# Joint 128-row transfers for the last 64 rows of the modulation and of wk, wv and wq

## The chip, the cores and the metric

The kernel runs on one core of one Trainium2 chip. The metric is the time of one execution on the device in microseconds (us), as the median of the runs shown. Three engines compute beside TensorE (PE): VectorE (DVE), ScalarE (ACT) and GpSimd (POOL). SyncE (SP) issues nearly all transfers; they go to the core's 16 DMA engines.

## The reference, cut to what matters

One transformer block over 2048 tokens of width D = 576. A row `c` of 576 numbers is turned into six rows of modulation by `w_mod` (576 x 3456). The first two of them shift and scale the normalised input, and q, k and v are products of the result with `wqkv` (576 x 1728).

```python
mod = (_silu(c) @ w_mod).reshape(c.shape[0], 6, 1, -1)
sa, ca, ga, sb, cb, gb = (mod[:, 0], mod[:, 1], mod[:, 2], mod[:, 3], mod[:, 4], mod[:, 5])
h = _layernorm(x, axis=-1) * (1 + ca) + sa
x = x + ga * _A_ref(h, A_wqkv, A_wo)      # linear attention, 32 heads of 18
h = _layernorm(x, axis=-1) * (1 + cb) + sb
x = x + gb * _B_ref(h, B_w1, B_w2)        # silu MLP, 576 -> 4608 -> 576
```

The change concerns the start alone: the product with the first two pieces of `w_mod`, and the loads of `wqkv`.

## The kernel before

**Rows of 576.** 576 is 4 x 128 + 64, so each weight comes as four chunks of 128 rows and a tail of 64. Each float32 operand is split into a rounded part (`hi`, made by ACT in `w_hi`) and the rest (`lo`, made by DVE or POOL in `w_lo`), and a product takes three passes of PE: hi by hi, lo by hi and hi by lo. Of a tail of 64 rows hi and lo lie in one tile of 128 partitions, so that two passes do.

**The first stage.** `load_mod_cols` loads the first two pieces of `w_mod` in two sets of columns (0 to 255, then 256 to 575): four chunks of 128 rows, which hold both pieces, and the tail, whose 64 rows of piece 0 go to partitions 0 to 63 of `tmod` and those of piece 1 to partitions 64 to 127, with one transfer each. DVE sums the four chunks weighted by silu(c) (`mod_sum`), PE adds the tail (`mod_tail`) and the partitions (`mod_sums`, `mod_last`), and `col_a` takes shift and scale. The row c itself comes by two small loads on ACT's queue: 4 rows of 128 (L277), and its last 64 numbers twice, as a transfer of 1 x 2 x 64 (L278). Meanwhile the first four row tiles of x (`xt`, 128 tokens each) are normalised, turned by PE, modulated and split (`modulate`, `split_h`) into `hT`.

`load_w(j, ks)` loads wk (j = 0), wv (1) and wq (2) into `acc`, chunk by chunk; chunk k = KC = 4 is the tail of 64 rows, loaded by `load_rows` into partitions 0 to 63 of a tile of its own. Then ACT and DVE split them. PE makes k of the row tiles 0 and 1 (`k_part`, into `psK`), then v of tile 0 (`v_proj`), v of tile 1, then q of tiles 0 and 1, and from there on k, v and q tile by tile. The last two lo parts of wv that v of tile 0 waits for (chunk 3 and tail) are made by POOL.

**What sets the order.** PE's order in this stage is that of the code. For the other engines a scheduler orders the instructions, and the tables `ORDERS` (one for each engine, read by `arrange`) put the first 547 instructions of DVE, the first 425 of ACT, the first 119 of POOL and the first 153 of SP of the traced program in a given order. Each engine takes its instructions strictly in that order. The MLP's main part is ordered by a plan of its own.

**The tail's lines.** L293 loads the tail of the modulation, L236 the chunks of the weights, L238 their tails; L317 and L318 are `w_hi` of a chunk and of a tail, L323 and L325 `w_lo` of a chunk and of a tail.

Of the kernel before, what the change touches and what calls it, by code (L numbers as in the profile page):

```python
# [17 lines left out]
P = 128  # L18
# [5 lines left out]
def kernel(ctx: ExitStack, tc, A_x, A_wqkv, A_wo, B_x, B_w1, B_w2, c, w_mod, out):  # L24
# [7 lines left out]
    nc = tc.nc  # L32
    V, A, G, T = nc.vector, nc.scalar, nc.gpsimd, nc.tensor
# [3 lines left out]
    S, D = x.shape  # L37
# [6 lines left out]
    KC = D // P  # L44
# [3 lines left out]
    HALF = D // 2  # L48
# [4 lines left out]
    def f32(ap):  # L53
        return ap.bitcast(F32)
# [3 lines left out]
            0-106 114 107-109 115 110-113 116-1159 1162 1160 1163 1161 1164-2530  # L58
        """,
        "DVE": """  # L60
            0 3 2 1 4 6-7 11 8 12-13 9-10 14-16 18 17 5 19-22 30 23-24 28-29 25-27 43 31 44 33-34 36 35 37-38 32 39 41
            40 42 45-47 50 48-49 67-68 51-53 57 70 62 64 69 58-59 63 65 122 85-86 66 71-72 87 55 88 73 60 74 61 76-77
            75 78-79 89-90 56 80 83 81-82 91 84 123 54 93 97 96 98 100 94 99 92 124 95 101 103-104 107-108 105 102 125
            109-110 132-133 135 134 111 138 136-137 139 106 112 141-142 140 143-144 114 145-146 148-149 117 147 113
            115 126 118-119 116 120 128-129 131 121 192 150 195 193 196 151 194 198 130 199 152 158 153 197 201 200
            202-203 154 157 204 161 208 127 155 205 159 206 209 160 162 164 156 207 175-176 165 168 163 169 166 170
            177 171 178 173 172 167 179 174 182-183 185-186 184 187-188 191 189 210 216 211 190 219 212 215 213 217
            214 220 218 228-229 232 231 225 180 233 223 235 234 230 236 239 237 240 221 241 238 222 242 224 243
            245-247 244 248 251-252 249 253 250 227 254 257 255 258 256 226 261 259 262 265 267 266 268-270 263 260
            271-272 264 273-274 278-279 275-276 280-281 277 282 284 283 285-286 288-289 296 290-294 297 308-309 298  # L70
            295 299 317 300-301 318 302 310 312 311 327 303 287 328 313 336 319 314 337 320-322 315 181 304 329-330
            323-325 346 326 331-332 316 338 340 347 339 333 358 341 305 345 359 334 370 335 352 349 342-343 350-351
            356 371 348 379 344 306 353 307 354 360 380 362-363 390 361 355 368 364-365 391 372 366 373 369 374 367
            378 409 381-382 357 388 383 410 375 384 426 376 385 387 389 395-396 394 377 398 392 399 403 397 405 402
            386 393 415 413-414 427 416 400 417 406 401 418 435 423 428 424 407 425 419 429-430 436 408 420-421 434
            431 422 411 432 437 412 438 404 439 444 446-448 440 433 441 445 442 457 450-451 443 452-455 449 459 456
            460-462 466 463 458 465 467-468 482 469 471 486 483 473 464 488 470 489 472 494-495 484 496-497 491 485
            475 498 490 478 499 492 501 506 500 476-477 479 503 502 493 474 481 505 480 504 510 507 511 487 509 508
            513-514 516 512 515 517-521 523 522 524 527 525-526 529 528 532-533 531 540 536 535 537 534 541 538-539
            543-544 542 530 546 545  # L80
        """,
        "Activation": """
            0-2 4-6 9 7-8 10 3 11-12 16 19 13-14 18 17 15 21 26 20 27 22-23 29 24 28 25 30-31 35 32-33 36-37 46 48 39
            47 42 49 40 44 50 41 55 43 58 56-57 38 59-60 45 53 61 51 54 52 62 34 65 63 66-70 64 72 71 73-74 77-78 75
            79-82 76 83-85 93-96 87 86 98 88 99 101 100 97 89 102 104 90-91 103 92 105-107 111-113 108 116 109 117-118
            120 114 110 115 121 145-146 119 122 151 126-127 147 123-124 148 144 128-129 152 131 143 130 149 125 134
            132-133 135-136 150 154 153 138-139 137 140-141 160 155 161-162 156 142 165 157 166-167 158 168 163 159
            164 169-170 179 176-177 180-181 178 182 184-186 183 175 187-188 190 189 191-192 171 193-195 173 196 172
            197-198 200 199 201-203 205 174 206 204 208 210 209 207 212 211 213-217 219-220 222-223 218 221 225-226
            224 228 227 229-233 237 236 238 234 239-241 235 245-247 242 251 258 243 252 248-249 253 264 259 250 260  # L90
            271 254 256 261 265-266 257 255 262 267 269-270 274 272 268 283 263 276 275 294 273 278 277 279 297
            280-281 284-285 244 282 290-291 304 292-293 295-296 288 286-287 320 289 298-302 307 309-310 308 311 303
            305 312 323-324 313 316 331 314 306 317 315 319 327-328 332-333 329 318 330 334-335 326 336 321 325 322
            337 339 341-343 340 338 344-345 349-350 346-348 351 353 352 354-355 367 357 356 359 369 360 366 363 374
            361 364 375 358 362 371 380 365 381 377 372 382 376 383 378 373 379 368 384 370 386 385 390 387-388 392
            391 393 396 398 397 395 401 389 399-400 403-404 394 405 402 408 406 414 410-411 407 416 415 418 412 421
            417 422 419-420 409 413 424 423
        """,
        "Pool": """
            7-10 0 3 2 4-6 11-15 18 16-17 21 19-20 22 25 23 27 26 24 28-30 36 32 31 34 33 37 35 39 38 42 40 44 46 43  # L100
            45 41 48 51 47 49 53 55 52 54 50 66 56-57 69 58 61-62 59 67 65 63 71 60 70 68 72 64 73 75 74 80 85 81-82
            76-77 84 78 83 91 79 90 93 86 92 95-98 94 89 99 101 87 100 102 104 103 106 88 105 108 111 110 113 107 114
            109 116-117 112 115 118
        """,
        "SP": """
            0-25 30-31 26 28 27 29 32 39 33-34 40-43 35-38 53 44 71 54 72-73 55-56 45 74 46 58 47-48 57 59-60 75 61 77
            76 78 62 49 81 63-65 79 82-83 80 86 52 89 92 85 87 84 66 91 96 90 93 97-98 95 69 50 88 51 94 104 99 105
            101 67 100 103 70 102 107 68 109 108 114 106 110-111 116 113 115 118 124 117 119-121 126-127 123 112 122
            125 128 131 129 133 132 134-135 130 136-137 139 148 141 138 140 142-144 147 145-146 149-152
        """,  # L110
    }

# [33 lines left out]
    cols = {n: const.tile([P, KC + 1, 2], F32, name=f"col_{n}") for n in ("a", "b")}  # L146
# [6 lines left out]
    acc = [accb[t // 4][:, t % 4, :] for t in range(NT)]  # L153
# [14 lines left out]
    wq = wqp.tile([P, 2 * KC + 1, D], F32R, name="wq")  # L168
# [65 lines left out]
    def load_rows(raw, src, k):  # L234
        if k < KC:
            nc.sync.dma_start(raw, src[k * P : (k + 1) * P, :])  # L236
        else:
            nc.sync.dma_start(raw[0:64], src[KC * P : D, :])  # L238
# [49 lines left out]
    def load_mod_cols(k0, k1):  # L288
        c0, c1 = k0 * P, min(k1 * P, D)
        for k in range(KC):  # L290
            if k == 2:
                for a in range(2):
                    nc.sync.dma_start(tmod[a * 64 : a * 64 + 64, 0, c0:c1], w_mod[KC * P : D, a * D + c0 : a * D + c1])  # L293
            src = w_mod[k * P : (k + 1) * P, 0 : 2 * D].rearrange("p (a d) -> p a d", a=2)
            nc.sync.dma_start(mods[k][:, :, c0:c1], src[:, :, c0:c1])

    def load_w(j, ks):
        for k in ks:
            load_rows(acc[5 * j + k], A_wqkv[:, (D, 2 * D, 0)[j] :][:, 0:D], k)

    load_mod_cols(0, HEAD)
    load_w(0, range(HEAD))
# [12 lines left out]
    def w_hi(wpart, k, full):  # L315
        if k < KC:
            return A.copy(wpart(k), full)  # L317
        return A.copy(wpart(2 * KC)[0:64], full[0:64])  # L318

    def w_lo(wpart, k, full, eng=V):  # L320

        if k < KC:
            return eng.tensor_sub(wpart(KC + k), full, f32(wpart(k)))  # L323
        else:
            return eng.tensor_sub(wpart(2 * KC)[64:128], full[0:64], f32(wpart(2 * KC)[0:64]))  # L325

    def split_w(wpart, k, full, eng=V):
        w_hi(wpart, k, full)
        w_lo(wpart, k, full, eng)
# [92 lines left out]
    with tc.manual_schedule(engines={mybir.EngineType.PE}):  # L422
# [83 lines left out]
        w_lo(wv_, 0, acc[5], V)  # L506
        w_lo(wv_, 1, acc[6], V)
        a0 = k_phi(kps[0])
        for k in range(2, KC + 1):
            w_hi(wv_, k, acc[5 + k])  # L510
        w_lo(wv_, 2, acc[7], V)
        pool = [w_lo(wv_, k, acc[5 + k], G) for k in (3, 4)][-1]
        first = *k_split(0, a0), pool
        after = *k_split(1, k_phi(kps[1])), pool

# [158 lines left out]
    with tc.manual_schedule(engines={mybir.EngineType.PE}):  # L674
        for t in range(NT):
# [4 lines left out]
            if t > 1:  # L680
                k_proj(t)
            if t == 1:
                for k in START:
                    split_w(wqp_, k, acc[10 + k], V)
                plane_room = accp.tile([P, 8 * D], U16, name="acc3")
            if more and i == 1:
                ln = LayerNorm(pa)
# [44 lines left out]
    with tc.manual_schedule(engines={mybir.EngineType.PE}):  # L732
# [75 lines left out]
        for j in range(KC + 1):  # L808
# [16 lines left out]
            if j in (0, 2):  # L825
                r = rooms[j // 2]
# [818 lines left out]
```

## Time and profile before

| | before |
|---|---|
| median of 3 runs (lowest to highest) | 1131.22 us (1130.78 to 1131.24) |
| the profiled execution | 1129.66 us |
| its span, first to last instruction | 1127.8 us |
| PE busy in the span | 1115.3 us (99%) |
| DVE, ACT, POOL busy | 976.8, 554.5, 657.2 us |

The profiled execution lasts 1.86 us longer than its span and is 1.56 us under the median of the runs. Busy time is that of instructions that compute; an engine that waits is idle, and one that issues transfers (SP all the time) is shown under its name with a q. Where a group says "L238" it is the line of the kernel before.

### The profile page before, as it was taken

The numbers are of one execution on the slowest core, as the hardware profiler recorded it, in microseconds if no ns is written. First come the engines' busy times: TensorE is split into PE (matmuls) and PEld (weight loads), VectorE is DVE, ScalarE is ACT, GpSimd is POOL, SyncE is SP. The second block draws the span as 40 slices with busy tenths as digits, with TensorE's granted clock in tenths as the row PEclk, the third lists the DMA queues.
The fourth block names the chain that finished last, engine by engine and source line by source line (L and its number), as shares of the span: only waits on it lengthen the run. The fifth ranks groups of instructions, "written<-read, shape, count | busy, mean of one in ns | idle before, by whom it ended". The sixth has DMA issues, their size and how long they took to land.

```text
span 1127.8 us, 19241 instructions
## 1 busy us (share of the span) xinstructions
PE 1115.3 (99%) x6961; PEld 1029.8 (91%) x6961; DVE 976.8 (87%) x1554; ACT 554.5 (49%) x1139; POOL 657.2 (58%) x733
## 2 busy tenths in 40 slices
PE   8999999999999999999999999999999999999998
PEld 7999999999989899999999999999999999999998
DVE  7776655678978899999999999999999999999996
ACT  5646763555556444444445444444454454444441
POOL 1102010544734787677766775777677757776786
PEclk9999999999999999999999999999999999999999
DMA  9326620313388796977977969779769788797674
GB/s 287 118 70 141 136 48 20 85 48 121 143 310 320 291 331 261 354 267 261 358 268 269 349 259 338 290 257 347 276 256 361 261 323 302 258 350 273 250 306 158
DMA packets 76529, 274.03 MB, mean 243 GB/s; under 512 B 22543, under 2 KB 38676, under 8 KB 53396
## 3 DMA queue, kind: packets, MB, share of 16 engines
q1 hardware_dynamic: 76424, 272.80, 67.5%
q8 instruction: 56, 0.92, 0.3%
q14 instruction: 37, 0.30, 0.1%
q10 hardware_dynamic: 12, 0.00, 0.0%
HBM read 251.31 MB, written 17.08 MB: 238 GB/s over the span
## 4 chain that ended last, share of the span: by engine, by line
PE 91%; DVE 3%; DMA 2%; ACT 2%; SPq 1%; POOL 1%; issue 1%; POOLq 0%; DVEq 0%; ACTq 0%
PE up L1376 34%; PE down L1449 32%; PE psK L232 12%; PE big L232 5%; PE big L946 2%; PE small L935 1%; PE kvp L608 1%; PE big L858 1%; PE up L1479 1%; PE down L1479 1%; DMA raw<-in_B_w_dram 1%; DMA acc<-in_A_wqkv_dram 1%; PE small L220 0%; DMA acc<-mf 0%; ACT H L205 0%
## 5 line engine op out<-in xcount | busy, mean ns | idle before, releaser
L1457 DVE TENSOR_TENSOR acc<-down,acc 128x576 f32<-128x576 f32 x330 | 245.9, 753 | 12.0 <-PE down L1449 2.1
L1376 PE MATMUL up<-hT,w 128*128 128x512 f32 x916 | 239.3, 390 | 0.0
L1376 PEld LDWEIGHTS up<-hT,w 128*128 128x128 f32 x916 | 164.5, 188 | 24.7
L1411 POOL TENSOR_TENSOR s<-f,f 128x256 f32<-128x256 f32 x66 | 51.7, 784 | 155.3 <-ACT f L1392 155.3
L1449 PE MATMUL down<-w,hb 128*128 128x288 f32 x792 | 120.6, 294 | 0.0
L1449 PE MATMUL down<-w,hc 128*128 128x288 f32 x792 | 120.6, 294 | 0.0
L1449 PEld LDWEIGHTS down<-w,hb 128*128 128x128 f32 x792 | 113.7, 188 | 5.3 <-DVE acc L1457 0.2
L1449 PEld LDWEIGHTS down<-w,hc 128*128 128x128 f32 x792 | 113.8, 188 | 5.1
L1457 DVE TENSOR_TENSOR U<-down,U 128x576 f32<-128x576 f32 x132 | 99.6, 754 | 17.9 <-PE down L1449 16.0
L127 DVE TENSOR_TENSOR w<-v,w 128x288 fp32r<-128x288 f32 (+1 forms) x170 | 114.2, 680 | 0.1
L232 PE MATMUL psK<-w,hT 128*128 128x352 f32 (+3 forms) x506 | 105.5, 336 | 1.2 <-POOL w L325 0.6
L1376 PE MATMUL up<-room,w 128*128 128x512 f32 x348 | 91.1, 390 | 0.5 <-DVE f L1397 0.5
L1430 POOL TENSOR_TENSOR hc<-s,hc 128x512 fp32r<-128x512 f32 x66 | 89.4, 1354 | 1.1 <-ACT hc L1426 1.1
L1392 ACT ACTIVATE f<-f 128x512 f32<-128x512 f32 x102 | 64.5, 632 | 50.6 <-DVE f L1397 28.0
L232 PEld LDWEIGHTS psK<-w,hT 128*128 128x128 f32 x506 | 81.8, 189 | 7.5 <-POOL w L325 0.8
L1395 DVE TENSOR_TENSOR f<-up,p 128x512 f32<-128x512 f32 x102 | 69.7, 683 | 12.0 <-PE up L1376 11.4
L1376 PEld LDWEIGHTS up<-room,w 128*128 128x128 f32 x348 | 62.5, 188 | 10.3 <-DVE f L1397 1.0
L1115 ACT CAST w<-v 128x288 fp32r<-128x288 f32 x85 | 36.8, 434 | 70.7 <-PE down L1449 58.5
L1415 POOL TENSOR_TENSOR f<-f,s 128x256 f32<-128x256 f32 x66 | 51.3, 777 | 34.4 <-DVE hb L1430 22.9
L190 POOL TENSOR_TENSOR rstd<-ve,neghalf 128x4 f32<-128x4 f32 (+3 forms) x10 | 9.0, 901 | 93.7 <-DVE ve L189 93.7
L1449 PE MATMUL down<-w,hd 128*128 128x288 f32 x396 | 63.0, 294 | 0.0
L1449 PE MATMUL down<-w,ha 128*128 128x288 f32 x396 | 63.0, 294 | 0.0
(309 smaller groups left out, 2543.1 us busy)
## 6 DMA issues: line engine op xcount, KB each, us to landing
hT<-hd SPq DMA_DIRECT2D x66, 1280.0 KB
hT<-hd SPq DMA_DIRECT2D x45, 1024.0 KB
room<-hd SPq DMA_DIRECT2D x35, 1280.0 KB
room<-hd SPq DMA_DIRECT2D x20, 1024.0 KB
v<-in_B_w_dram SPq DMA_DIRECT2D x17, 576.0 KB
v<-in_B_w_dram SPq DMA_DIRECT2D x17, 512.0 KB
hd<-S SPq DMA_DIRECT2D x6, 1024.0 KB
xt<-in_A_x_dram SPq DMA_DIRECT2D x16, 288.0 KB
```

What stands on the lines that cost most here:

```text
L127: return V.tensor_sub(lo, full, f32(hi))
L232: T.matmul(ps, xpart(a), wpart(b), start=n == 0, stop=n == len(pairs) - 1)
L946: T.matmul(ps[:, h, :HALF], hs[:, j, a, tok], w2[:, j, b, h * HALF : (h + 1) * HALF], start=j == 0 and (a, b) == (0, 0), stop=j == G2 - 1 ...
L1115: A.copy(self.w2[n][:, 0], src)
L1376: T.matmul(ps, left, right, start=first and m == 0, stop=m == len(seq) - 1, skip_group_check=True)
L1392: A.activation(self.f[i, k], self.f[i, k], AF.Silu)
L1395: V.tensor_add(f, self.bank[bank[1]], self.p1)
L1411: G.tensor_add(self.s[:, 0:1], half(i, 0, 1), half(i, 1, 1))
L1415: G.tensor_sub(half(i, 1, 0), half(i, 1, 0), self.s[:, 1:2])
L1430: eng.tensor_sub(t[:, :, 1, :], src, f32(t[:, :, 0, :]))
L1449: T.matmul(ps[:, p, :HALF], self.a[i, n][:, u, p * P : (p + 1) * P], self.w.w2[n][:, v], start=n in (1, 5, 7, 6) and j == 0, stop=j == 2, ...
L1457: V.tensor_add(dst, ps[:, :, :HALF], dst)
```

## The change

The two loads of the modulation's tail become one: a source of 2 x 64 rows (piece, row) goes to the 128 partitions of `tmod`, for each set of columns. The tails of wk and wv, which are the same 64 rows and neighbouring columns of `wqkv`, become one transfer of 2 x 64 rows into partitions 0 to 127 of what was the tile of wk's tail; it stands after row tiles 2 and 3 of x, where wk's tail stood ahead of them and wv's tail after the last chunk of wv. The tail of wq comes as its left half (288 columns) in partitions 0 to 63 and its right half in 64 to 127, again by one transfer, after wq's four chunks. The bytes that are moved stay the same. `tail_hi` and `tail_lo` split what lies in the upper partitions; wq's tail takes two hi and two lo of 288 columns, not one of 576. The tables for DVE, ACT, POOL and SP are new, that for PE is not.

```diff
         "SP": """
-            0-25 30-31 26 28 27 29 32 39 33-34 40-43 35-38 53 44 71 54 72-73 55-56 45 74 46 58 47-48 57 59-60 75 61 77
...
+            0-15 17-18 16 19-22 28 23 25 24 26-27 29 36 30-31 37-38 32-35 39 68 50 40-41 52-53 51 69 42 70-71 43-45 54-56 72 49 57-58
...
             if k == 2:
-                for a in range(2):
-                    nc.sync.dma_start(tmod[a * 64 : a * 64 + 64, 0, c0:c1], w_mod[KC * P : D, a * D + c0 : a * D + c1])
+                both = w_mod[KC * P : D, 0 : 2 * D].rearrange("r (a d) -> a r d", a=2)
+                nc.sync.dma_start(tmod[:, 0, c0:c1], both[:, :, c0:c1])
...
         for k in ks:
-            load_rows(acc[5 * j + k], A_wqkv[:, (D, 2 * D, 0)[j] :][:, 0:D], k)
+            if k < KC:
+                load_rows(acc[5 * j + k], A_wqkv[:, (D, 2 * D, 0)[j] :][:, 0:D], k)
+            elif j != 1:
+                dst, cols = (acc[KC], slice(D, 3 * D)) if j == 0 else (acc[10 + KC][:, :HALF], slice(0, D))
+                tails = A_wqkv[KC * P : D, cols].rearrange("r (a d) -> a r d", a=2)
+                nc.sync.dma_start(dst, tails)
...
+    def tail_hi(w, full, a):
+        return A.copy(w[a * 64 : a * 64 + 64], full[a * 64 : a * 64 + 64])
+
+    def tail_lo(w, full, a, eng=V):
+        part = slice(a * 64, a * 64 + 64)
+        return eng.tensor_sub(w[64 - a * 64 : 128 - a * 64], full[part], f32(w[part]))
...
-        for k in range(2, KC + 1):
+        for k in range(2, KC):
             w_hi(wv_, k, acc[5 + k])
+        tail_hi(wv_(2 * KC), acc[KC], 1)
         w_lo(wv_, 2, acc[7], V)
-        pool = [w_lo(wv_, k, acc[5 + k], G) for k in (3, 4)][-1]
+        w_lo(wv_, 3, acc[8], G)
+        pool = tail_lo(wv_(2 * KC), acc[KC], 1, G)
...
-                for k in START:
+                for k in range(KC):
                     split_w(wqp_, k, acc[10 + k], V)
+                for a in range(2):
+                    w = wq[:, 2 * KC, a * HALF : (a + 1) * HALF]
+                    tail_hi(w, acc[10 + KC][:, :HALF], a)
+                    tail_lo(w, acc[10 + KC][:, :HALF], a)
```

On SP, at the program's start, the loads of the modulation stand as follows (- before, + changed; `hT` is the room of the modulation's chunks here, acc_95 the tile of wk's chunks):

```order
-L293 DMA tmod<-in_w_mod_dram 64x256 x2
+L293 DMA tmod<-in_w_mod_dram 128x1x256
 L295 DMA hT<-in_w_mod_dram 128x2x256 x2
 L236 DMA acc_95<-in_A_wqkv_dram 128x576 x2
 L295 DMA hT<-in_w_mod_dram 128x2x320 x2
-L293 DMA tmod<-in_w_mod_dram 64x320 x2
+L293 DMA tmod<-in_w_mod_dram 128x1x320
 L295 DMA hT<-in_w_mod_dram 128x2x320 x2
```

For each set of columns of the modulation two loads of 64 rows have become one of 128 (printed with its middle count of 1), at the same place among the loads of the chunks. A little further on in SP's order, behind the rows above, stand the weights' tails (acc_95 to acc_98 are the tiles of wk, wv and wq):

```order
 L236 DMA acc_95<-in_A_wqkv_dram 128x576 x2
-L238 DMA acc_96<-in_A_wqkv_dram 64x576
 L268 DMA xt<-in_A_x_dram 128x576 x2
+L304 DMA acc_96<-in_A_wqkv_dram 128x1x576
 L236 DMA acc_96<-in_A_wqkv_dram 128x576 x3
 L236 DMA acc_97<-in_A_wqkv_dram 128x576
-L238 DMA acc_97<-in_A_wqkv_dram 64x576
-L238 DMA acc_98<-in_A_wqkv_dram 64x576
```

The load of wk's tail is gone from ahead of the two row tiles of x, and that of wk's and wv's tails together stands behind them; the last two lines are the tails of wv and wq, of which the first is part of that load and the second comes after wq's four chunks now, as one transfer of 128 x 1 x 288.

On ACT, from the split of the modulated chunks 2 and 3 (L211) on, the rows are these: the hi of wk's tail (L318 before, L323 now), then that of wv's chunks 0 to 2 (L317, L322) among the normalising of row tile 2 (L197):

```order
 L211 CAST hT<-raw 128x256 x2
-L318 CAST w<-acc_96 64x576
-L317 CAST w<-acc_96 128x576
+L323 CAST w<-acc_96 64x576
+L322 CAST w<-acc_96 128x576
 L211 CAST hT<-raw 128x256
-L317 CAST w<-acc_96 128x576
+L322 CAST w<-acc_96 128x576
 L197 ACTIVATE xt<-xt,nm,rstd 128x64
 L197 ACTIVATE xt<-xt,nm,rstd 128x576
-L317 CAST w<-acc_96 128x576
+L322 CAST w<-acc_96 128x576
```

Nothing has moved here: the hi of wk's tail stands ahead of the same rows as before, in the queue of an engine that takes them one after the other, and it now reads what the joint transfer brings. The hi of wv's chunk 3 and of its tail follow further down, as before.

## Rows read from the trace of the kernel before

**Rows 1.** The page: busy time, and the granted clock in 40 slices.

```profile
PE 1115.3 (99%) x6961; PEld 1029.8 (91%) x6961; DVE 976.8 (87%) x1554; ACT 554.5 (49%) x1139; POOL 657.2 (58%) x733
...
PEclk9999999999999999999999999999999999999999
```

**Rows 2.** Busy time by stage; columns are in the first row.

```profile
core 0: us, PE busy (x) PEld busy (x) DVE busy (x) ACT busy (x) POOL busy (x), PEclk, DMA share, GB/s
...
6.00:12.00 6.00, 5.32 (x46) 4.92 (x45) 3.00 (x10) 2.21 (x4) 0.72 (x1) 1.00 0.99 323
12.00:18.00 6.00, 5.45 (x39) 4.69 (x38) 5.59 (x9) 3.64 (x9) 0.00 (x0) 1.00 1.08 314
...
24.00:32.00 8.00, 6.80 (x50) 6.22 (x49) 7.11 (x12) 7.97 (x16) 3.51 (x2) 1.00 0.66 206
32.00:50.00 18.00, 18.00 (x137) 18.00 (x138) 16.13 (x38) 9.96 (x24) 1.01 (x1) 1.00 0.39 132
50.00:120.00 70.00, 69.44 (x462) 65.61 (x461) 49.67 (x98) 44.66 (x77) 7.37 (x4) 1.00 0.45 110
120.00:1128.00 1008.00, 1000.70 (x6179) 921.16 (x6177) 888.14 (x1364) 479.29 (x1002) 640.38 (x710) 1.00 0.69 253
```

**Rows 3.** Waits of PE up to 45 us: total, times, longest.

```profile
PE psK L415 <- ACT hT L211: 1.3, 1, 1.3
...
PE kvp L379 <- DMA tmod<-in_w_mod_dram: 0.8, 2, 0.4
...
PE psK L232 <- POOL w L325: 0.6, 1, 0.6
```

**Rows 4.** The chain that ended last, up to 36 us: start, us, what.

```profile
3.58 0.59 SPq L293
...
5.87 5.87 DMA acc<-in_A_wqkv_dram
...
17.72 1.55 PE kvp L379 x12
...
22.11 0.57 ACT w L318
...
28.15 0.59 ACT w L318
...
29.81 2.01 POOL w L325
...
31.87 0.81 PE psK L232 x4
```

**Rows 5.** DMA up to 32 us: GB/s in slices, packets, queues, issues with KB each.

```profile
GB/s 0 0 75 354 344 194 237 335 319 300 235 302 339 360 383 303 299 330 371 396 259 256 326 320 386 392 389 277 179 225 268 233 262 386 398 318 127 66 0 0
...
q1 hardware_dynamic: 5328, 8.41, 86.6%
...
q10 hardware_dynamic: 12, 0.00, 0.0%
...
acc<-in_A_wqkv_dram SPq DMA_DIRECT2D x12, 288.0 KB
xt<-in_A_x_dram SPq DMA_DIRECT2D x6, 288.0 KB
hT<-in_w_mod_dram SPq DMA_DIRECT2D x4, 320.0 KB
hT<-in_w_mod_dram SPq DMA_DIRECT2D x4, 256.0 KB
...
acc<-in_A_wqkv_dram SPq DMA_DIRECT2D x3, 144.0 KB
tmod<-in_w_mod_dram SPq DMA_DIRECT2D x2, 80.0 KB
tmod<-in_w_mod_dram SPq DMA_DIRECT2D x2, 64.0 KB
```

**Rows 6.** ACT in order of time: the hi of wq's tail (start, us, what).

```profile
35.30 0.67 ACT L318 CAST wq<-acc 64x576 fp32r<-64x576 f32 x1
```

More of the change, by code (lines that the diff above doesn't have):

```diff
@@ L60 @@
         "DVE": """
[L61 to L80, printed above, removed]
+            0 3 2 1 4 6-7 11 8 12-13 9-10 14-16 18 17 5 19-22 30 23-24 28-29 25-27 43 31 44 33-34 36 35 37-38 32
@@ new lines @@
+            39 41 40 42 45-47 50 48-49 68-69 51-53 57 71 62-63 70 58-59 123 64 72 86 55 60 65-67 87-88 74 73 77 75-76 78
+            61 90 79-80 56 91 82 84 81 89 85 54 83 92 94 93 98 97 95 99 101 100 102 104 96 124 105 108 106 109 103 107
+            110 112 111 133 136 134-135 139-140 137-138 142 113 143 141 144-145 147-148 115 118 149-150 146 116 125
+            119-120 114 126-127 121 117 122 129 193 132 151 194 130 152 196 195 153 199 197-198 131 202 159 200 155
+            203 201 204 154 205 156 158 207 160 162 208 157 161 128 206 165 163 209 164 210 176 166 170 169 167 171
@@ new lines @@
+            177 172 178 174 168 173 179 183 186 184 187 180 188 185 175 189 192 217 211 190 212 220 191 213 216 218
+            214 222 221 224 219 215 229-230 233 232 234 236 235 231 225 237 223 238 240-242 239 243-244 246-248 245
+            249 226 252-253 228 250 227 254 251 255 181 258 256 262 259 263 257 260 266 268 270-271 267 269 261 264
+            272-273 265 275 279 276 274 277-278 280-281 283 282 284-287 289-290 297 291-292 298 309 293 310 299-300
+            318 301 319 328 311 294-295 313 312 306 329 182 302 296 314 288 337 305 320 338 321 303-304 347 322 317
@@ new lines @@
+            315-316 323-324 330 325-326 332 327 331 348 359 339-340 307 360 341 371 336 350 333 353 342 345 343 351
+            346 308 334 352 349 357 361 372 335 362 380 354 344 381 363 355 391 364 356 373 365 374 370 366-367 369
+            375 368 358 376 382 392 410 383 379 411 384-385 377-378 427 389 396 388 386 397 395 399-400 393 404 387
+            401 406 390 428 403 398 416 414-415 436 424 417-418 409 402 437 419 394 407 425 408 420 426 429-431 421
+            435 422-423 438-439 412-413 405 432 440 433-434 441-442 448 445-446 449 451 447 458 452-453 443-444 454
@@ L81 @@
+            459 455 450 460 457 461 456 467 462-464 466 468-470 465 483 472 487 484 474 489 471 490 495 473 507 497
+            485 478 498 496 492 491 480 499-500 486 502 476-477 479 482 504 501 475 481 505 503 506 509 494 488 508
+            493 512-513 510 514 511 515 517 516 520 518 521 519 523 522 524-526 528-529 527 531 541 530 532-534
+            537-538 535-536 540 542 544 543 545 547 539 546
         """,
         "Activation": """
-            0-2 4-6 9 7-8 10 3 11-12 16 19 13-14 18 17 15 21 26 20 27 22-23 29 24 28 25 30-31 35 32-33 36-37 46 48 39
@@ L84 @@
[L84 to L97, printed above, removed]
+            0-2 4-6 9 7-8 10 3 11-12 16 19 13-14 18 17 15 21 26 20 27 22-23 29 24 28 25 30-31 35 32-33 36-37 46
@@ new lines @@
+            48 39 47 42 40 44 41 38 56 49-51 59 43 60 57-58 34 45 61 52 62 54-55 53 63-64 66-67 70-71 68-69 65 73 72
+            74-75 78-79 76 82 77 83 80-81 84-86 95 94 96 88 100 97-98 89 102 87 90 101 103 105 104 91 99 92 106-107 93
+            108 112-114 109-110 117-118 115 119 116 111 121 144 122-123 146 120 127 124 128 147 125 129 151 130 152
+            132 145 149 131 133-135 126 150 148 153 136 154 137 155 139 138 140-142 161-163 156 166 143 157 167 158
+            168 159 164 169-171 160 165 180 177-178 181-183 185-187 179 184 188-189 191-192 190 193 175 194-196 174
@@ new lines @@
+            197-199 201 172-173 202 176 200 203-204 206-207 205 208-209 211 210 214 212-213 215-216 218 220-221 223
+            222 217 224 219 226-228 225 230 229 231-234 237-239 235 240-241 246 236 242 252 247 243 259 248 244
+            253-254 265 249-250 260 251 261 257 255 272 258 266 256 262 267 263 268 284 270 273 245 277 295 264 275
+            278 276 271 279-280 269 285-286 274 281-282 298 291-292 305 283 296-297 293-294 290 299-300 289 288 287
+            321 301 303 310 308 311 302 309 312 304 306 317 313 324 314 325 332 315 307 320 335 316 318-319 328-330
@@ L98 @@
+            333 331 334 336 323 326 322 337 327 338 340 342 346 341 344-345 343 347 350-351 339 349 348 352-355 367
+            356 358 357 360-361 364 362 365 359 369 375-376 368 366 363 381-382 370 377 373 378 372 371 383-384 380
+            379 386 385 387 391 388 374 392-393 389 398 397 396 400 390 394 401-402 404-406 399 403 415 395 408-411
+            407 412-413 419 417 414 416 420 422 418 421 423 425 424
         """,
         "Pool": """
-            7-10 0 3 2 4-6 11-15 18 16-17 21 19-20 22 25 23 27 26 24 28-30 36 32 31 34 33 37 35 39 38 42 40 44 46 43
@@ L101 @@
-            45 41 48 51 47 49 53 55 52 54 50 66 56-57 69 58 61-62 59 67 65 63 71 60 70 68 72 64 73 75 74 80 85 81-82
-            76-77 84 78 83 91 79 90 93 86 92 95-98 94 89 99 101 87 100 102 104 103 106 88 105 108 111 110 113 107 114
-            109 116-117 112 115 118
+            7-10 0 3 2 4-6 11-15 18 16-17 21 19-20 22-24 27 25-26 28 30 29 32 31 34 33 37 35 38-39 42 40 44 36 43 46
+            41 48 45 47 51 49 53 52 55 54 50 66 56 69 71 57-58 61-62 67 75 65 59 70 63 60 68 72 64 73-74 80-82 76 91
@@ L104 @@
+            77 84 78 83 79 93 90 95 86 92 96-99 94 101 100 88 103 105 85 104 102 108 110 106 89 87 111 113 107 114 109
+            115 112 116-118
         """,
         "SP": """
-            0-25 30-31 26 28 27 29 32 39 33-34 40-43 35-38 53 44 71 54 72-73 55-56 45 74 46 58 47-48 57 59-60 75 61 77
-            76 78 62 49 81 63-65 79 82-83 80 86 52 89 92 85 87 84 66 91 96 90 93 97-98 95 69 50 88 51 94 104 99 105
-            101 67 100 103 70 102 107 68 109 108 114 106 110-111 116 113 115 118 124 117 119-121 126-127 123 112 122
@@ L109 @@
-            125 128 131 129 133 132 134-135 130 136-137 139 148 141 138 140 142-144 147 145-146 149-152
+            0-15 17-18 16 19-22 28 23 25 24 26-27 29 36 30-31 37-38 32-35 39 68 50 40-41 52-53 51 69 42 70-71 43-45 54-56 72 49 57-58
+            74 73 75 59-60 46 80 78 61 76 62 48 77 79 88 63 86 89 83 65 84 47 90 66 81-82 87 93 92 85 94 91 95 97 100
+            102 96 99 101 67 64 98 106 104-105 107 103 108 112 109 111 114 113 110 115 118 116 120 123 121 117 119 124
+            122 125-128 131 129-130 132-134 136 138 135 137 139 145 140 144 141-143 147 146 149 148
```

## The prediction

> **What bounds the kernel now.** I read the page first: PE is busy for 1115.3 of 1127.8 us, at the full granted clock in all 40 slices [rows 1]. Next, the busy time by stage: PE has no idle time from 32 to 50 us, 0.56 us of it from 50 to 120 and 7.3 us in the 1008 us after that [rows 2]. So a delay of PE before 32 us is not made good later: it moves the end by as much. Then the chain up to 36 us, which tells what sets PE's progress there [rows 4]: SP's issues up to 5.87 us, the landing of wk's second chunk at 5.87 + 5.87 = 11.74, sums of the modulation up to PE's L379 at 17.72, and from about 21 us on ACT, piece after piece: at 22.11 the hi of wk's tail, at 28.15 that of wv's tail, then POOL with wv's last two lo parts, and at 31.87 PE, which had waited 0.6 us for POOL [rows 3]. ACT is busy 7.97 of the 8 us from 24 to 32 [rows 2], and the transfers keep all 16 DMA engines busy from 6 to 18 us, 0.99 to 1.08 of their time [rows 2]. The reader is to see that two things run in a fixed order side by side, the DMA engines' queue and ACT's, and that the tail's hi is where ACT's meets the load that has been changed.
>
> **On how many engines a load runs.** The packets tell it. Of the loads of [rows 5], 33 on SP's queue have landed by 32 us: 12 chunks and 6 tiles of x of 128 pieces, 8 of the modulation of 2 x 128, and 7 of 64. That makes 18 x 128 + 8 x 256 + 7 x 64 = 4800 pieces, and the queue shows 5328: 528 more, which is 33 x 16. I read them as one note of completion from each engine that took part, so that a load of 64 rows ran on 16 engines just as one of 128. ACT's queue (q10) shows 12 packets for its two loads of c, whose outer counts are 4 and 2: 6 pieces, so 6 notes, 4 and 2. A load's outer count thus limits its engines. The joint loads have 128 on the side of the tile and 2 on that of the source (piece or half first, then row). No row of this trace has sides that differ. At one end the load is spread over 16 engines and costs what it did; at the other it runs on 2. I take 2, since the row nearest in the count that is small, the 1 x 2 x 64 load, had 2, and a split into 16 equal shares would have to cut the source inside its 2.
>
> The Trainium skill (DMA: Bandwidth & Descriptors, "Why a DMA increments its semaphore by 16 and not by 1") states that a load is divided among the largest number of engines, at most 16, that divides the outermost count above one of both its sides. By it the joint loads have 2 engines and the sum below stands; by an even spread the time is that of the first rival. The counts 16, 4 and 2 above agree with it, as far as they go.
>
> **The sum.** Every other load needs all 16 engines, two of them included, and each engine works through its queue in order; so I follow one of the two. KB are those of [rows 5], 1024 bytes.
>
> Before, an engine had carried a sixteenth of 2 tiles of x, 4 first chunks and 2 first tails of the modulation and 2 chunks of wk at 11.74: (2 x 288 + 4 x 256 + 2 x 64 + 2 x 288)/16 = 144 KB, 8 of them of the tails. Changed, one of the two carries until wk's tail has landed a sixteenth of 4 tiles of x, 4 + 4 chunks of the modulation and 4 of wk, (8 x 288 + 4 x 256 + 4 x 320)/16 = 288 KB, and half of three joint loads, 64 + 80 + 144 = 288 KB.
>
> Left after 11.74 are 288 - 136 = 152 KB of ordinary loads and 288 - 8 = 280 KB of joint ones. Ordinary at 314 GB/s over 16, 19.6 GB/s an engine (12 to 18 us): 7.9 us. Joint at a rate between 323/16/0.99 = 20.4 (6 to 12 us) and 253/16/0.69 = 22.9 (the long stage) [rows 2]: 14.1 or 12.5 us; I take 13.3, since neither is a row of two engines alone. wk's tail lands at 11.74 + 7.9 + 13.3 = **32.9**.
>
> Its hi stood at 22.11, and ACT was not waiting for the load then: it is now **10.8 us** later, with all that ACT does behind it, 9.76 us of it up to PE's 31.87. The two modulation loads on their own would be later by (56 + 70) KB at the mean joint rate, 21.6 GB/s: 6.0 us, at L379; ACT would then come to the tail at 28.1 and still wait, so that this part lies inside the 10.8.
>
> What is late next. wv's four chunks follow at 72 KB, 3.8 us: 36.7, and the last is wanted just ahead of 28.15 + 10.8 = 38.9. wq's tail follows them by 90 KB of ordinary loads and 72 of its own, 4.7 + 3.4 us: 44.8, wanted at 35.30 + 10.8 = 46.1 [rows 6]. Both fit, the second by 1.3 us; if it came later, ACT would hold back what stands behind it. wq's tail now takes two hi and two lo instead of one each: one more ACT piece of at most 0.67 us [rows 6] and one of DVE, both beside a PE that is busy for 18.00 of 18 us while ACT is for 9.96 [rows 2]; without that cover they would cost their length once. Three fewer issues save SP 0.59 us each or so [rows 4], of which one lay ahead of the landing at 11.74; with two engines in arrears it is worth 0, and otherwise at most 0.59. The new tables further on could win or lose at what PE idles after 50 us, 7.9 us in all; no row tells which, so 0, with 1.3 us to either side, the longest single wait of PE in the first stage [rows 3].
>
> The profiled execution of 1129.66 us becomes 1140.5. It lay 1.56 us under the median of the runs, which by the same sum goes from 1131.22 to **1142.0**.
>
> Bounds: all 442 thousand bytes (432 KB) left at the fastest slice, 398/16 = 24.9 GB/s [rows 5], land at 29.5, 7.4 us late; at 314/16/1.08 = 18.2, at 36.0, 13.9 us late. With the tables' 1.3 the forecast's own range is 1137 to 1147.
>
> **The rivals.** *The joint loads are spread over 16 engines.* Then an engine carries 288 + 36 KB to the tail, and what is left at 11.74, 180 KB at 19.6, lands at 21.1, just ahead of 22.11. The queue moves the same bytes; the issue saved is worth up to 0.59 us, PE's waits for the modulation's tail 0.8 [rows 3]: 1130.6, and 1129.8 at best, not slower. For it speaks that 64-row loads had 16 engines too; against it the 2 notes of the 1 x 2 x 64 load. It is decided by the number of engines: with n of them the tail lands at 11.74 + 7.9 + (576/n - 8) KB at 21.6 GB/s, that is 22.7 for 8, 26.1 for 4; from 8 on nothing can be measured.
>
> The same page of the Trainium skill (DMA: Bandwidth & Descriptors, "Rules for kernel authors") advises for this very case one transfer to 128 partitions in place of two to its halves, because both halves use the same 16 engines and so run one after the other. By that advice the change is of the right kind, and the time that of this rival; the 16 notes of each 64-row load show its premise.
>
> *Two engines, and PE's clock falls in the stall.* PE's longest wait in the first stage is 1.3 us [rows 3] and its granted clock is the upper level, 2.4 GHz, throughout [rows 1, 2]. The stall would be several times as long. If PE then worked at 1.2 GHz up to 31.87 + 10.8, its 6.8 us of [rows 2] in the 8 us to 32 would take 13.6: 5.6 us more, 1147.6. Against it: the most of that work waits for ACT anyway.
>
> *The stall is there, but small.* If two engines alone move their pieces much faster than any row shows, or four engines carry the load, the tail lands near 26 and the time is about 1135.
>
> **How the numbers follow.** Forecast 0.75, spread 0.16, fallen clock 0.06, small stall 0.03. The time is the forecast's, 1142. From 1135 to 1149 lie about all of the forecast, the fallen clock and half of the small stall: 0.82; the rest is nearly all the first rival, 4 us below, and is left out. Runs of this kernel tell 0.2%, 2.3 us, from no change. Slower by more is all but the spread, 0.84; of the spread most is the same, 0.13, and 0.03 faster, where tables and issue would have to win together.
>
> **What the changed profile would show.** Fewer packets on SP's queue for the same pieces: 2 notes for each joint load, not 16. A DMA share well below 0.99 from 8 to 33 us. In ACT's rows a wait for the load of wk's tail of 4 to 5 us, its hi near 33, and PE's L232 after POOL near 42.7. PE's idle time grows by about 11 us before 45 us and not after 50. Wrong I would be if the joint loads showed 16 notes, or if ACT did not wait ahead of the tail's hi; half wrong if the wait is there and PE makes some of it good, or if wq's tail holds ACT a second time.

## The result, and the profile after

The changed kernel takes 1143.2 us (median of 4 runs, 1142.39 to 1143.82) where the kernel before takes 1131.0 (4 runs beside them, 1130.16 to 1131.24): a ratio of 1.0114, with a 95% interval of 1.0102 to 1.0125. It is slower by 12.2 us; 1142 were forecast. The page of the changed kernel, its span, PE's busy time, PE's granted clock in 40 slices and SP's queue:

```profile
span 1140.3 us, 19257 instructions
...
PE 1119.7 (98%) x6961; PEld 1032.8 (91%) x6961; DVE 975.4 (86%) x1555; ACT 554.8 (49%) x1140; POOL 652.3 (57%) x733
...
PEclk9899999999999999999999999999999999999999
...
q1 hardware_dynamic: 76384, 272.80, 66.7%
```

The clock has a slice of 8 where [rows 1] has none. The queue moved the same 272.80 MB in 76,384 packets; before, the page had 76,424. That gives the number of engines without a guess. The four joint loads of the whole program make 4 x 128 pieces, the seven loads that they replace 7 x 64 pieces and 7 x 16 notes, 560 packets together. 560 - 40 = 520 = 4 x (128 + 2): two notes for each joint load, so two engines.

The same stages as in [rows 2], shifted where the work has shifted (busy time of each engine, granted clock, DMA share, GB/s):

```profile
6.00:12.00 6.00, 4.18 (x32) 3.96 (x31) 3.05 (x9) 1.31 (x2) 0.73 (x1) 1.00 0.97 296
12.00:18.00 6.00, 4.40 (x36) 4.09 (x35) 3.98 (x8) 4.11 (x7) 0.00 (x0) 1.00 0.97 299
18.00:24.00 6.00, 4.82 (x38) 4.58 (x39) 3.20 (x5) 2.21 (x6) 0.00 (x0) 1.00 0.59 179
24.00:32.00 8.00, 3.80 (x28) 3.37 (x27) 2.84 (x11) 2.92 (x8) 0.81 (x1) 0.95 0.69 190
32.00:43.00 11.00, 9.22 (x56) 9.20 (x57) 9.31 (x14) 10.54 (x21) 2.91 (x2) 0.73 0.50 162
...
110.00:131.00 21.00, 17.93 (x115) 16.56 (x114) 15.44 (x34) 15.25 (x25) 3.71 (x2) 1.00 0.37 100
```

Up to 18 us the DMA engines are about as busy as before (0.97, where a share well below 0.99 was foretold from 8 us on); then the share drops. PE loses time in two places: up to 43 us, which was forecast, and 3.07 of 21 us from 110 to 131, which was not; between them it is idle for 0.45 us. PE's waits up to 45 us (total, times, longest), the counterpart of [rows 3], and, first from the kernel before and then from the changed one, ACT's rows of the hi parts that [rows 4, 6] show:

```profile
PE psK L427 <- DVE w L330: 4.7, 1, 4.7
PE kvp L391 <- DMA tmod<-in_w_mod_dram: 4.4, 2, 2.6
```

```profile
22.01 0.67 ACT L318 CAST w<-acc 64x576 fp32r<-64x576 f32 x1
```

```profile
30.72 0.67 ACT L323 CAST w<-acc 64x576 fp32r<-64x576 f32 x1 [4.63 <-DMA acc<-in_A_wqkv_dram]
...
37.10 0.67 ACT L333 CAST w<-acc 64x576 fp32r<-64x576 f32 x1
...
46.76 0.88 ACT L333 CAST wq<-acc 64x288 fp32r<-64x288 f32 x2
```

wk's tail stands at 30.72, behind a wait of ACT of 4.63 us for its load; it stood at 22.01 (22.11 is its start in the chain of [rows 4]), so it is 8.7 us late. wv's tail (37.10) and wq's (46.76, now two of 288 columns) have no wait of their own. PE's products behind POOL's last lo, at 31.87 in [rows 4], stand at 41.01: 9.1 us later.

Where the rest went is followed by one product, `kvp<-pk,vx`, which PE makes again and again in this stage, at the same places of its order in all kernels here. The columns are its first, third, fifth, sixth and seventh start after 50 us in the kernel before, and one near 187, in us (with the difference to before):

| kernel | first | third | fifth | sixth | seventh | a later one |
|---|---|---|---|---|---|---|
| before | 53.52 | 79.14 | 103.44 | 116.42 | 128.52 | 187.49 |
| changed | 63.73 (+10.2) | 89.34 (+10.2) | 113.80 (+10.4) | 128.41 (+12.0) | 141.49 (+13.0) | 200.45 (+13.0) |
| change, old tables (e8) | 62.81 (+9.3) | 88.42 (+9.3) | 112.73 (+9.3) | 125.52 (+9.1) | 137.62 (+9.1) | 196.82 (+9.3) |
| before, new tables (e7) | 54.35 (+0.8) | 79.97 (+0.8) | 104.41 (+1.0) | 119.91 (+3.5) | 132.01 (+3.5) | 190.95 (+3.5) |

So the loss is made in two steps, ahead of 64 us and between 114 and 142 us, and next to nothing is won back (13.0 us there, 12.5 at the span's end). Each row is one execution: the profile of e4 below, whose median is that of before, is 1.0 us late in the first column (54.51), so a difference of 1 us in one row says little.

### The profile page after: what moved, and what is told of

Its sections match the earlier page's. It is cut to its first block, busy times and chain, and to the rows that moved or that the text cites. A ratio compares the mean times of both kernels' runs of the same rounds, so it can differ in the third digit from the quotient of the medians.

```text
span 1140.3 us, 19257 instructions
## 1 busy us (share of the span) xinstructions
PE 1119.7 (98%) x6961; PEld 1032.8 (91%) x6961; DVE 975.4 (86%) x1555; ACT 554.8 (49%) x1140; POOL 652.3 (57%) x733
## 3 DMA queue, kind: packets, MB, share of 16 engines
q1 hardware_dynamic: 76384, 272.80, 66.7%
## 4 chain that ended last, share of the span: by engine, by line
PE 80%; ACT 1%; DVE 1%; issue 0%; POOL 0%; ACTq 0%; POOLq 0%
PE up L1394 34%; PE down L1467 32%; PE big L232 6%; PE small L953 2%; PE big L964 2%; PE big L876 1%; PE psK L232 1%; PE small L220 1%; PE up L1497 1%; PE down L1497 1%; ACT xn L197 0%; PE psK L834 0%; PE small L1158 0%; DVE nm L191 0%; POOL rstd L190 0%
## 5 line engine op out<-in xcount | busy, mean ns | idle before, releaser
L1475 DVE TENSOR_TENSOR acc<-down,acc 128x576 f32<-128x576 f32 x330 | 245.7, 753 | 12.2 <-PE down L1467 2.6
L232 PE MATMUL psK<-w,hT 128*128 128x352 f32 (+3 forms) x506 | 105.7, 337 | 0.0
L232 PEld LDWEIGHTS psK<-w,hT 128*128 128x128 f32 x506 | 82.1, 189 | 6.2 <-issue 0.2
L190 POOL TENSOR_TENSOR rstd<-ve,neghalf 128x4 f32<-128x4 f32 (+3 forms) x10 | 10.4, 1040 | 101.5 <-DVE ve L189 101.5
```

Source lines behind the costliest of these rows:

```text
L232: T.matmul(ps, xpart(a), wpart(b), start=n == 0, stop=n == len(pairs) - 1)
L1475: V.tensor_add(dst, ps[:, :, :HALF], dst)
```

## The experiments

Theory: the two engines of the joint loads cost nearly all of it (the tail lands late, PE cannot catch up). First rival: what the joint load does otherwise (its new places, more issues' worth in one, the order) costs it. Second rival, once the second step was seen: the new tables cost a part. Interval means the 95% interval of the ratio to the kernel before.

**Joint loads as halves again (e1, e5, e6).** e1 makes every joint load two loads of 64 rows, all else as changed; e5 does so for the modulation alone (the edit shown), e6 for the weights alone.

```diff
-                both = w_mod[KC * P : D, 0 : 2 * D].rearrange("r (a d) -> a r d", a=2)
-                nc.sync.dma_start(tmod[:, 0, c0:c1], both[:, :, c0:c1])
+                for a in range(2):
+                    nc.sync.dma_start(tmod[a * 64 : a * 64 + 64, 0, c0:c1], w_mod[KC * P : D, a * D + c0 : a * D + c1])
```

> The changed kernel, but each of its four joint loads issued as two loads of 64 rows to the same places; SP's table gets the second half right behind the first, all else is the changed kernel's. Theory (a joint load runs on two DMA engines): the hi of wk's tail is back at about 22 to 23 us on ACT (30.7 in the changed kernel), PE's L232 after POOL near 32 (41.0), the packets of SP's queue up to 32 us show 16 notes a load; time 1131 if the 3.1 us that PE waits for DVE near 110 us come from the lateness, 1134 if they come from the new tables. Rival (the order is to blame: wk's tail behind two tiles of x and joined with wv's, and the tables): still 1141 to 1143.

> The changed kernel with only the modulation's two joint loads issued as two each; those of the weights stay joint. Theory (two engines): 56 + 70 KB less on each of the two, wk's tail lands near 25, ACT waits some 3 us for it; with 0 to 3 us near 110 us, 1134 to 1137. If only the modulation's loads mattered: 1131 to 1134.

> The changed kernel with only the weights' two joint loads issued as two each; the modulation's stay joint. Theory (two engines): PE's sums of the modulation 4 us late as in the changed kernel (21.7 against 17.7), ACT comes to wk's tail near 26 and finds it landed; with 0 to 3 us near 110 us, 1135 to 1138. If only the weights' loads mattered: 1131 to 1134.

Measured: e1 1133.57 us (ratio 1.0029, 1.0017 to 1.0041), e5 1137.67 (1.0066, 1.0051 to 1.0081), e6 1138.29 (1.0067, 1.0050 to 1.0083). With e1 wk's tail hi is back at 22.12 without a wait, and 8.7 of the 12.2 us are gone, but not all: 3.5 us over before stay in a kernel without any joint load. e5 and e6 show that each pair of joint loads delays the tail by about half: 26.79 in e5, where ACT waits 4.06 us for the tail's load, and 27.21 in e6, without a wait there, since all of ACT's work comes late behind the modulation (the 12 products of L379, at 17.72 in [rows 4], stand at 22.64 in e6). Alone 4.8 and 5.2 us late, together 8.7: they nearly add up, as they would if all joint loads use the same two engines; which engines they use is not shown. The times of e5 and e6 are 0.7 and 0.3 us above the ranges expected.

**The number of engines alone (e2, e3, e4).** The kernel before, with its loads of 64 rows, its order and tables; only the source is told in another way, as n x (64/n) rows (the tails' rows then stand in another order, so that the output is not the reference's).

```diff
-            nc.sync.dma_start(raw[0:64], src[KC * P : D, :])
+            nc.sync.dma_start(raw[0:64], src[KC * P : D, :].rearrange("(r n) d -> n r d", n=2))
```

(and the same for the modulation's tail; n = 2 in e2, 4 in e3, 8 in e4.)

> The kernel before with its own seven loads of 64 rows, order and tables, but each source told as 2 x 32 rows (even rows, then odd ones), so that its outermost count is 2; rows of the tails meet other columns, so the output is not the reference's. Theory (outermost count of the source sets the number of engines, 2 here): a wait of ACT for wk's tail or wv's tail, 7 to 10 us lost by 42 us, 1138 to 1141, 2 notes for each such load. Rival (the order or the tables are to blame): 1131, no wait.

> The kernel before with each tail's source told as 4 x 16 rows (every fourth row first; the output is not the reference's). Theory (outermost count sets the engines, 4 here): 4 notes a load; an engine of the four has 54 KB more for the modulation's tails, 2.5 us at 21.6 GB/s, and 27 KB more for wk's: 2.5 to 4 us lost, 1132.5 to 1134. Rival (a load of 64 rows has 2 engines or 16): as with 2, 1138, or as before, 1130.

> The kernel before with each tail's source told as 8 x 8 rows (every eighth row first; the output is not the reference's). Theory: 8 notes a load, 18 KB more on each of eight engines for the modulation's tails, 0.8 us: 1130 to 1131.5. Rival (any split source is slow, whatever its count): 1138 as with 2.

| source's outermost count | packets of SP's queue, whole run | 76,424 less these, over 7 loads | wk's tail hi at | us | ratio (interval) |
|---|---|---|---|---|---|
| 64 (before) | 76,424 | 0 | 22.01 | 1130.07 and 1130.34 | |
| 8 (e4) | 76,368 | 8 | 22.99 | 1130.37 | 1.0001 (0.9992 to 1.0011) |
| 4 (e3) | 76,340 | 12 | 22.76 | 1132.02 | 1.0012 (1.0002 to 1.0021) |
| 2 (e2) | 76,326 | 14 | 26.87 | 1137.95 | 1.0069 (1.0054 to 1.0084) |

Each load has lost 8, 12 and 14 of its 16 notes: it ran on 8, 4 and 2 engines, just the count told. Nothing else was changed, and the time follows: 7.9 us for two engines, 1.7 for four (both less than expected), none for eight. In e2 the tail's hi is 4.9 us late, and the wait of ACT that was expected is only one of 0.2 us at wv's tail; the product of the table above is 7.1 us late at its first start after 50 us (60.62). That is the mechanism shown by itself, and the first rival falls for these loads. Two engines show directly in the changed kernel, in a stretch in which nothing else moves (columns as in the stages above):

```profile
30.00:30.50 0.50, 0.00 (x0) 0.00 (x0) 0.00 (x0) 0.00 (x0) 0.00 (x0) 1.00 0.13 51
```

0.13 is 2 of 16 engines, at 51 GB/s or 25.5 each, and all the compute engines stand still. The other 14 had nothing to do, because SP itself stood ahead of its next loads:

```profile
SPq L236 <- DMA acc<-in_A_wqkv_dram: 5.6, 2, 5.2
```

A semaphore is a counter that a finished load raises. In the trace these loads take eight of them in turn, and each waits for the load eight places ahead of it: the one issued at 30.71 us waits for the joint load of wk's and wv's tails, issued at 14.85. It is a wait of the program.

**The tables (e7, e8, e9).** e7 is the kernel before, its code and loads, with the tables of the change (renumbered, since the change traces other instructions); e8 is the change with the tables of before; e9 is e8 with the joint loads as halves, so that only the tails' new places and wq's two hi and lo are left.

```diff
         "SP": """
-            0-25 30-31 26 28 27 29 32 39 33-34 40-43 35-38 53 44 71 54 72-73 55-56 45 74 46 58 47-48 57 59-60 75 61 77
+            0-25 30-31 26 28 27 29 32 39 33-34 40-41 35-38 42 71 53 43-44 55-56 54 72 45 73-74 46-48 57-59 75 52
...
```

> The kernel before, its code and its seven loads of 64 rows in their old order, but with the changed kernel's tables for DVE, ACT, POOL and, behind the first loads, SP (places shifted to the code before). Theory (what is left in the changed kernel with halved loads, 3.5 us, comes from the new tables): 1133 to 1134, with PE waits for DVE's lo of v near 40 and near 110 us. Rival (it comes from the tails' new places): 1130 to 1131.

> The changed kernel with its joint loads in their order, but with the tables of before for DVE, ACT, POOL and, behind the first loads, SP. Theory (two engines cost 8 to 9 us by 42 us, the new tables 3 more): 1139 to 1140. Rival (lateness alone makes both losses): 1143 as the changed kernel.

> The change with both of its costly parts taken out: every joint load issued as two loads of 64 rows, and the tables of before. What is left is the tails' new places in the tiles and the one more hi and lo of wq. Theory (two engines 9.3 us, tables 3.0 us, nothing else): 1130 to 1131, no wait of ACT for wk's tail, whose hi stands near 22.1. Rival (the new places cost something of their own, or the two costs only add up by chance): 1132 or more.

Measured: e7 1133.38 (1.0026, 1.0016 to 1.0036), e8 1139.66 (1.0083, 1.0068 to 1.0098), e9 1130.2 beside 1130.05 (1.0002, 0.9993 to 1.0011). That makes the account: 9.3 us for the two engines and the new places together, of which the places are 0.2 (not to be told from nothing), and 3.0 for the tables; 12.3 together, 12.2 measured. The second rival is right for a quarter of the loss, and e8's row in the table above is flat at 9.1 to 9.3 from its first column on.

What the tables do shows on SP near 88 us: first the kernel before, then e7, start, length and what is issued.

```profile
87.34 1.22 SPq L268 DMA_DIRECT2D xt<-in_A_x_dram  x2
88.60 4.69 SPq L660 DMA_TRANSPOSE raw<-acc  x2
```

```profile
88.99 6.27 SPq L663 DMA_TRANSPOSE raw<-acc  x3
95.32 0.58 SPq L271 DMA_DIRECT2D xt<-in_A_x_dram  x1
```

Two row tiles of x went ahead of two transposes, and now go behind three. The statistics of x on DVE wait for it, and PE's products behind `vx`, in e7:

```profile
98.79 0.46 DVE L187 BATCH_NORM_STATS2 st<-xt 128x6 f32<-128x288 f32 x1 [3.26 <-DMA xt<-in_A_x_dram]
```

```profile
107.27 5.48 PE L235 MATMUL psK<-wq,hT 128*128 128x288 f32 x28 [1.73 <-DVE vx L130]
```

and in the kernel before, where the same 28 products take 3.96 us:

```profile
104.42 3.96 PE L232 MATMUL psK<-wq,hT 128*128 128x288 f32 x28
```

PE waits 1.73 us, and then its 28 products take 1.5 us more: the granted clock is 0.73 from 107 to 108 us, 0.50 from 108 to 110, the lower of its two levels (1.2 of 2.4 GHz), 0.56 in the next and 1.00 from 111 on, against 1.00 throughout in the kernel before. The changed kernel has the same wait of DVE, 10 us later, and PE's behind it:

```profile
108.80 0.46 DVE L184 BATCH_NORM_STATS2 st<-xt 128x6 f32<-128x288 f32 x1 [3.88 <-DMA xt<-in_A_x_dram]
```

```profile
117.27 3.96 PE L232 MATMUL psK<-wq,hT 128*128 128x288 f32 x28 [2.33 <-DVE vx L127]
```

Here PE waits longer, but its clock stays at 1.00 and the 28 products take their 3.96 us; two more waits for `vx` (0.34 and 0.73 us) stand ahead of the same 28 products at other row tiles. So the tables' 3 us are not made in the same way in e7 and in the changed kernel, and the sum of 12.3 agrees in part by chance.

**The two tiles of x alone (e10, e11).** e10 is the kernel before with these two tiles behind three transposes; e11 is e7 with them ahead of two of the transposes again.

```diff
 e10, on the table of before:
-            ... 53 44 71 54 72-73 55-56 45 74 46 ...
+            ... 53 44 71 55-56 54 72 45 73-74 46 ...
 e11, on the new table:
-            ... 42 71 53 43-44 55-56 54 72 45 73-74 46-48 ...
+            ... 42 71 53 43-44 54 72-73 55-56 45 74 46-48 ...
```

> The kernel before, with that one group of SP's issues in the new order: three transposes ahead of the second and third of four x tiles near 90 us. Theory: DVE waits 3 to 5 us for x near 93 to 98 us, PE loses 1 to 3 us there and its clock falls below 1.00 for some slices; 1132 to 1135. Rival (the order of these issues matters only together with the engines' new orders, or not at all): 1130.3.

> Loads and code of before with the new tables, but on SP the two x tiles near 95 us again ahead of two of the transposes, as before. Theory (the 3 us of the new tables come from these tiles: DVE's BN_STATS waits 3.3 us for one, PE then for vx, and its clock falls): the wait is gone, PE's granted clock stays at 1.00 from 90 to 130 us, and the time is 1130.3 to 1131.3. Rival (the engines' own new orders cost it): 1133 to 1133.5 as with all the new tables.

Measured: e10 1131.65 (1.0013, 1.0005 to 1.0022), e11 1132.40 (1.0019, 1.0009 to 1.0028). Both fall between theory and rival. The order of two issues is enough to lose 1.6 us; the wait it was expected to make is there:

```profile
96.25 1.18 DVE L185 BATCH_NORM_STATS2 st<-xt 128x6 f32<-128x288 f32 x3 [3.47 <-DMA xt<-in_A_x_dram]
```

But the clock did not fall in e10, and with the tiles back in e11 the 3.0 us of e7 become 2.4, each beside its own runs of the kernel before: only 0.7 us is won, and the intervals of e7 and e11 overlap. In e11's profile the wait of DVE is down to 0.96 us and the clock is 1.00 throughout, yet PE still waits twice for `vx`, 1.1 us at the longest, near 107 and 121 us, and by the table's first column (55.48) it has lost 2.0 us. Of these, 1.2 cannot come from the edit, which begins later than that (e7 has lost 0.8 there); this execution, of 1133.37 us, was 1.0 us above e11's median. So of the tables' 3.0 us the place of these two loads costs 1.6 by e10 and 0.7 by e11, a quarter to a half; the rest lies elsewhere in the new tables of the four engines, and which rows of them cost it is not shown.

**One joint transfer on 16 engines (e12).** As e8, but row first, then piece, in the source: the outermost count is 64.

```diff
-                both = w_mod[KC * P : D, 0 : 2 * D].rearrange("r (a d) -> a r d", a=2)
+                both = w_mod[KC * P : D, 0 : 2 * D].rearrange("r (a d) -> r a d", a=2)
...
-                tails = A_wqkv[KC * P : D, cols].rearrange("r (a d) -> a r d", a=2)
+                tails = A_wqkv[KC * P : D, cols].rearrange("r (a d) -> r a d", a=2)
```

> The joint loads stay single transfers, but row first, then piece, on the source's side, so that its outermost count is 64 and not 2; tables of before. Output is not the reference's, since the rows of the tails stand in other partitions. Theory (the source's outermost count sets the number of engines): the load is spread over 16, wk's tail hi near 22.1 without a wait, 1129.5 to 1130.8; by 32 us 16 notes for each of the three joint loads then landed. Rival (a joint load is slow because it fills 128 partitions from one issue, however its source is told): as with two engines, ACT waits near 4 us and the time is near 1139.

Measured: 1130.47 (1.0000, 0.9991 to 1.0009); wk's tail hi at 22.17, without a wait. The rows then stand in other partitions, so that the output is not the reference's. The queue shows 76,440 packets, 56 more than the changed kernel: 4 loads x 14 notes. So a joint load is not slow in itself; the two engines are all of it. It is not faster than before either, though SP issues fewer loads.

## Why the prediction was right, point by point

**Two engines.** Right, and the step that everything hung on. The 64-row loads with 16 notes and the 1 x 2 x 64 load with 2 [rows 5] were the evidence; 40 packets fewer in the run, and e2, e3, e4 and e12, show that the smaller of the two sides' outermost counts set it in each of them, up to 16. The Trainium skill states this rule (DMA: Bandwidth & Descriptors, "Why a DMA increments its semaphore by 16 and not by 1"), and these runs agree, with 8, 4 and 2 notes. The advice on the same page of the Trainium skill ("Rules for kernel authors") to take one 128-partition transfer for two halves would have given the first rival; it cost 9.3 us here, and with the source's rows outermost (e12) it gained nothing.

**The landing of wk's tail.** Right in kind, 2.2 us too late: the hi was put at 32.9 and stands at 30.72. The term that was mis-sized is the rate of the two engines: the sum moves 432 KB on each by 32.9, 20.9 GB/s, and the same KB by 30.72 are 23.3 (an estimate from the sum's own KB). The joint loads were taken at 21.6, between two rows in which all 16 work; two engines alone move 25.5 each, as the stretch of 51 GB/s above shows, above the 24.9 that was the fastest in the bounds. At 25.5 the 280 KB take 11.24 us, not 13.3, and the sum gives 30.9; but that rate is read only from 28.7 to 30.7 us, with the other 14 engines idle, and what the joint loads had before that is not shown. ACT's wait was foretold as 4 to 5 us and is 4.63.

**Modulation alone 6.0 us late.** Too much: PE's 12 products of L379, at 17.72 before, stand at 21.69 in the changed kernel, 4.0 us late, and at 22.64 in e6, where these loads alone are joint, 4.9 us late. (56 + 70) KB at 25.5 would take 5.1 us. ACT came to the tail at 26.1, not 28.1, and still waited, so that the part does lie inside the whole.

**What is late next.** Right: wv's and wq's tails have no wait. PE's L232 behind POOL was put at 42.7 and stands at 41.01. SP's three issues, and wq's one more hi and lo, were put at nothing; e9 (1.0002) and e12 (1.0000) agree.

**The tables at 0, with 1.3 us to either side.** Wrong, and the larger error: 3.0 us by e7, 3.5 by e1. "PE's idle time grows before 45 us and not after 50" failed with it: 3.07 us were idle from 110 to 131 us. The order showed two of x's loads behind three transposes, and [rows 2] showed that PE has next to no idle time there, but no row had a price, and the longest wait of the first stage was not a bound for a stage with other waits. It is also a term of the clock in e7, some 1.5 of the 3.0, though not in the changed kernel.

**The sum.** 10.8 + 0 became 9.3 + 3.0: the first term was 1.5 us too much and the second 3.0 too little. That 1142.0 came within 1.2 us of 1143.2 is in part luck, since the two errors are of opposite sign.

**The fallen clock.** The rival's mechanism was there: PE stood from 29 to 33.8 us, and its granted clock was 0.50, 1.2 GHz, from 32 to 38 us and 1.00 from then on (the last row at the low level, then POOL's last lo):

```profile
37.00:38.00 1.00, 1.00 (x6) 0.98 (x6) 1.00 (x3) 0.86 (x3) 0.84 (x1) 0.50 0.14 50
```

```profile
38.71 1.43 POOL L337 TENSOR_TENSOR w<-acc,w 64x576 fp32r<-64x576 f32 x1
```

It cost little. From 33.78 to 41.01 PE had no wait, and it came to its products behind this lo at 41.01, while the lo was done at 40.14: 0.9 us at most went to the clock there. 5.6 us had been its price; as the prediction held against it, PE waited until 33.78 whatever its clock. The fall does show in the sign of "about 11 us": PE's idle time up to 45 us grew from 4.81 us to 11.69, by 6.9, and the other 2.2 of the 9.1 us passed with PE busy at the low clock, where at the full one it would have waited for POOL's lo.

## What to carry to other kernels

Before two loads are joined, look at the outermost count on both sides of the new transfer: with 2 on the source's side it ran on 2 engines, though the tile's side had 64 or 128, and a load of 288 KB became the slowest thing in the queue. Put the rows outermost, which changes the partitions they go to, or leave the two loads of 64 rows, which cost nothing here (e9). Count packets in the whole run to see it: pieces are known, and what is left are the notes, one for each engine that took part. And where the engine that bounds the kernel has no idle time, a new order is not free: read from the order which loads moved behind which, and give that a price of its own in the sum.

## What was not expected

Two engines alone move 25.5 GB/s each; with all 16 at work it was 18 to 20 (296 GB/s at a share of 0.97 is 19.1; the stages of [rows 2] give 18.2 and 20.4).

While one slow load is under way, the issuing of others can stop: SP waited 5.2 us for that load's semaphore before it issued the load eight places behind it, and 14 engines stood idle. Whether that cost time of its own here, no run shows.

After a wait of PE of 1.73 us the clock fell near 108 us in e7, and after one of 2.33 us at the same product it stayed at 1.00 in the changed kernel. What else decides it, these runs do not show.
